# Two load queues, per-bank copies and a moved bias at the start of a squared-ReLU MLP kernel

## The chip, the cores and the metric

One core of one Trainium2 chip runs the whole kernel. The metric is the device time of one execution in microseconds. "Span" is the same execution as the profiler sees it, from the first to the last instruction; it is about 1.8 us shorter than the time. Starts and landings are the trace's; the recorded prediction gives a few of them 0.01 us higher.

## The reference, cut to what matters

```python
# x (1, 2048, 576), w1 (576, 4608), b1 (4608), w2 (4608, 576), b2 (576), all bf16
h = jnp.einsum("bsd,df->bsf", x, w1) + b1
r = jnp.where(h > 0, h, 0)
h = r * r
out = jnp.einsum("bsf,fd->bsd", h, w2) + b2
```

## The kernel before

The kernel works on four blocks of 512 rows. The first product needs x with its 576 columns on the partitions. For the later blocks a transposing DMA brings x in that way. For block 0 there is no time for that, so TensorE itself transposes x. This is the start of the kernel:

```python
WARM = [512] * 6 + [128]                 # matmuls on constants, while the loads run
for i, n in enumerate(WARM):
    keep(nc.tensor.matmul(wps[:, 0:n], lhsT=ones[:, 0:P], rhs=ones[:, 0:n], start=True, stop=True))
# ... (cut)
load_x(nc.sync, 0)                       # x0: 128 rows of x, 144 KB
load_x(nc.scalar, 1)                     # x1
load_w1n(nc.sync, 0)                     # w1k0: 128 rows of w1, the first 512 columns, 128 KB
load_x(nc.scalar, 2)                     # x2
load_w1n(nc.sync, 1)                     # w1k1
load_x(nc.sync, 3)                       # x3
for k in range(2, NK):
    load_w1n(nc.sync, k)                 # w1k2, w1k3
# ... identity; b1 (as 36 rows) and a column of b2 come on GpSimd's own queue; ScalarE's table load (cut)

# order on TensorE in block 0 ("k_outer"):
for j in range(2):                       # x0, x1
    for k in range(NK):
        x_transpose(j, k)
for j in range(2):
    x_transpose(j, NK)
x_copies(0)                              # PSUM -> SBUF, shared by VectorE and ScalarE
part(0, 0)                               # 4 matmuls of 256 columns with w1k0
for k in range(NK + 1):
    x_transpose(2, k)                    # x2
part(0, 1); part(0, 2)                   # w1k1, w1k2
for k in range(NK + 1):
    x_transpose(3, k)                    # x3
x_copies(1)
dup_windows(0)                           # two copies of 64x2048 on VectorE
part(0, 3)                               # w1k3
part(1, 0)
make_b1T()                               # b1 transposed on TensorE
for k in range(1, NK):
    part(1, k)
# ... then 4 matmuls of 64 rows ("pair", tile pn), and the row groups (tile ph), 512 columns each
```

I call the four column slices of w1 w1k0 to w1k3 and the four row tiles of x x0 to x3, as the change does. In the profile the x tiles are `x_sb`, the slices `w1n`, the other pieces of w1 `w_h`, the transposed tiles in PSUM `tb`, the first sums `pn`, and the row groups `ph`.

## Time and profile before

| | before |
|---|---|
| time, median of 3 first runs | 291.02 us (290.59 to 291.36) |
| span of the profiled execution | 289.6 us |
| first transpose / first row-group matmul / last matmul (starts) | 3.77 / 10.29 / 286.66 us |
| clock at full speed from | 6.51 us |

From the page of the kernel before, the header, the busy times and the chain that ended last (its two lines give shares of the span by engine and by source line), then two groups of the start (busy time and mean ns of one, then idle time of the engine before them):

```profile
span 289.6 us, 4693 instructions
PE 285.5 (99%) x2027; PEld 139.9 (48%) x2032; DVE 78.6 (27%) x176; ACT 96.7 (33%) x154; POOL 2.3 (1%) x10
...
PE 98%; DMA 1%; issue 0%; DVE 0%
...
L227 PE MATMUL pn<-xTw,w1n 128*128 128x256 bf16 x32 | 4.6, 295 | 0.0
...
L149 PE MATMUL tb<-ident,x_sb 128*128 128x128 bf16 x20 | 2.4, 288 | 0.2 <-DMA x_sb<-in_x_dram 0.2
```

TensorE is the bound, over the whole span, and the 32 first matmuls (L227) never waited. Busy PE is a weak sign, because matmuls are pipelined and their ends modelled, so I read the starts instead. This is the order in time on PE at the start (start, duration, what, how many; in brackets the idle time before and what ended it):

```profile
3.77 1.25 PE L149 MATMUL tb<-ident,x_sb 128*128 128x128 bf16 x10 [0.17 <-DMA x_sb<-in_x_dram]
4.87 1.01 PE L227 MATMUL pn<-xTw,w1n 128*128 128x256 bf16 x4
5.68 0.74 PE L149 MATMUL tb<-ident,x_sb 128*128 128x128 bf16 x5
6.21 1.19 PE L227 MATMUL pn<-xTw,w1n 128*128 128x256 bf16 x8
7.24 0.44 PE L149 MATMUL tb<-ident,x_sb 128*128 128x128 bf16 x5
7.51 1.04 PE L227 MATMUL pn<-xTw,w1n 128*128 128x256 bf16 x8
8.39 0.22 PE L166 MATMUL b1T_ps<-ident,b_rows 128*128 128x128 bf16 x1
```

After the wait for x0 there is no bracket, so no wait. The single starts behind these lines are 107 ns apart for transposes and 213 ns for 256 columns until 6.51 us, then 56 and 109 ns: the clock doubles. The Trainium skill ("TensorE: Matmul & The Clock Gate", Part 1) says that the clock starts at half speed and is released by a free-running activity window of about 3.4 us. The doubling in this trace agrees.

The loads, from the page (KB each, median us from issue to landing):

```profile
w1n<-in_w_dram SPq DMA_DIRECT2D x4, 128.0 KB, 3.9
x_sb<-in_x_dram ACTq DMA_DIRECT2D x2, 144.0 KB, 2.9
x_sb<-in_x_dram SPq DMA_DIRECT2D x2, 144.0 KB, 3.4
```

The trace's semaphore events give each landing: x1 at 3.52, x0 3.73, x2 4.13, w1k0 4.32, w1k1 5.86, x3 6.07, w1k2 6.47, w1k3 7.05 us.

### The profile page before, as it was taken

To read this page: it belongs to the slowest core of one execution; us is meant where nothing else is said; L and a number is where in the kernel's file an instruction comes from. 1 tells how busy PE (TensorE), PEld (TensorE's weight loads), DVE (VectorE), ACT (ScalarE), POOL (GpSimd) and SP (SyncE) were. 2 spreads that over 40 slices of the span, in tenths; PEclk is the share of its full clock that TensorE was granted. 3 is DMA by queue.
4 is the path that set the end of the run, shared out by engine and by line. 5 is a ranking of instruction groups with operands and counts; after the bars stand their busy time and mean duration, and the time that the engine had idled before them with its cause. 6 is when DMAs were issued, how large, how long until landed. Compare 5 with 4: busy or idle time off the path is not lost.

```text
span 289.6 us, 4693 instructions
## 1 busy us (share of the span) xinstructions
PE 285.5 (99%) x2027; PEld 139.9 (48%) x2032; DVE 78.6 (27%) x176; ACT 96.7 (33%) x154; POOL 2.3 (1%) x10
## 2 busy tenths in 40 slices
PE   8999999999999999999999999999999999999996
PEld 5544444444444555555544444444444455555555
DVE  1644554444500200000015444444440001100001
ACT  2566666666500000000027666666670000000000
POOL 3000000000000000000000000000000000000000
PEclk9999999999999999999999999999999999999999
DMA  7999999400001200000000000000000110000000
GB/s 198 221 245 188 308 389 212 92 0 2 0 14 25 52 16 18 16 16 18 16 16 2 1 2 0 2 0 2 0 2 0 36 38 16 16 16 19 33 16 18
DMA packets 31605, 16.52 MB, mean 57 GB/s; under 512 B 15700, under 2 KB 31584, under 8 KB 31584
## 3 DMA queue, kind: packets, MB, share of 16 engines
q1 hardware_dynamic: 31232, 15.91, 22.3%
q10 hardware_dynamic: 288, 0.30, 0.4%
q8 instruction: 16, 0.26, 0.4%
q14 instruction: 5, 0.04, 0.0%
q0 software_dynamic: 64, 0.01, 0.0%
HBM read 11.36 MB, written 2.36 MB: 47 GB/s over the span
## 4 chain that ended last, share of the span: by engine, by line
PE 98%; DMA 1%; issue 0%; DVE 0%
PE ph L188 42%; PE po L289 38%; PE pt L270 11%; PE pn L209 4%; PE pn L227 1%; DMA x_sb<-in_x_dram 1%; PE tb L149 1%; PE ph L190 1%; PE pn L203 1%; DVE o_sb L291 0%; PE b1T_ps L166 0%; PE pn L205 0%
## 5 line engine op out<-in xcount | busy, mean ns | idle before, releaser
L190 PE MATMUL ph<-xTw,w_h 64*128 64x512 bf16 x576 | 124.6, 376 | 0.0
L188 PE MATMUL ph<-xTw,w_h 64*128 64x512 bf16 x576 | 124.6, 376 | 0.0
L289 PE MATMUL po<-w_sb,hT 128*128 128x448 bf16 (+2 forms) x612 | 109.4, 341 | 0.0
L176 ACT ACTIVATE r<-ph,b1T 128x512 bf16<-128x512 f32 x128 | 81.1, 685 | 41.6 <-PE ph L190 41.6
L188 PEld LDWEIGHTS <-w_h 64*128 64x128 bf16 x576 | 54.1, 94 | 68.3
L289 PEld LDWEIGHTS <-hT 128*128 128x128 bf16 x612 | 58.5, 98 | 51.0
L177 DVE TENSOR_TENSOR hT<-r 128x512 bf16<-128x512 bf16 x144 | 61.2, 426 | 75.9 <-ACT r L176 75.5
L190 PEld LDWEIGHTS <-w_h 64*128 64x128 bf16 x576 | 54.1, 94 | 0.0
L291 DVE TENSOR_TENSOR o_sb<-po,b_bc 128x448 bf16<-128x448 f32 (+2 forms) x17 | 10.2, 597 | 125.8 <-PE po L289 125.8
L270 PE MATMUL pt<-hT,w_sb 128*128 128x512 bf16 x142 | 31.3, 379 | 0.1
L176 ACT ACTIVATE r<-pn,b1T 128x512 bf16<-128x512 f32 x16 | 10.3, 688 | 61.0 <-PE pn L205 59.6
L270 PEld LDWEIGHTS <-w_sb 128*128 128x128 bf16 x144 | 14.1, 98 | 17.0
L273 ACT ACTIVATE oT<-pt,b2T 128x512 bf16<-128x512 f32 x4 | 2.8, 688 | 28.3 <-PE pt L270 28.3
L209 PE MATMUL pn<-xTw,w1n 128*128 128x512 bf16 x45 | 10.4, 379 | 0.4 <-issue 0.3
L209 PEld LDWEIGHTS <-w1n 128*128 128x128 bf16 x48 | 4.5, 98 | 6.0 <-issue 0.8
L227 PE MATMUL pn<-xTw,w1n 128*128 128x256 bf16 x32 | 4.6, 295 | 0.0
L63 PE MATMUL wps<-const-bfloat16-1.0 128*128 128x512 bf16 (+1 forms) x7 | 2.8, 582 | 0.8 <-PEq L344 0.8
L227 PEld LDWEIGHTS <-w1n 128*128 128x128 bf16 x32 | 3.3, 107 | 0.5
L156 DVE COPY xTw<-tb 128x256 bf16<-128x256 bf16 x4 | 1.1, 292 | 6.7 <-PE tb L149 6.7
L119 DVE COPY xTw<-xTw 64x2048 bf16<-64x2048 bf16 x4 | 2.8, 690 | 0.2
L120 DVE COPY xTw<-xTw 64x2048 bf16<-64x2048 bf16 x4 | 2.7, 687 | 0.1
L149 PE MATMUL tb<-ident,x_sb 128*128 128x128 bf16 x20 | 2.4, 288 | 0.2 <-DMA x_sb<-in_x_dram 0.2
(23 smaller groups left out, 15.2 us busy)
## 6 DMA issues: line engine op xcount, KB each, us to landing
w_sb<-in_w_dram SPq DMA_DIRECT2D x4, 1296.0 KB, 12.7
w_h<-in_w_dram SPq DMA_DIRECT2D x14, 288.0 KB, 6.2
out_dram<-o_sb SPq DMA_DIRECT2D x15, 112.0 KB, 1.7
w_h<-in_w_dram SPq DMA_DIRECT2D x4, 144.0 KB, 3.5
w1n<-in_w_dram SPq DMA_DIRECT2D x4, 128.0 KB, 3.9
out_dram<-ot SPq DMA_DIRECT2D x4, 128.0 KB, 2.0
x_sb<-in_x_dram ACTq DMA_DIRECT2D x2, 144.0 KB, 2.9
x_sb<-in_x_dram SPq DMA_DIRECT2D x2, 144.0 KB, 3.4
```

The lines of the kernel that those rows point to most:

```text
L63: keep(nc.tensor.matmul(wps[:, 0:n], lhsT=ones[:, 0:P], rhs=ones[:, 0:n], start=True, stop=True))
L149: keep(nc.tensor.transpose(bank[:, slot, qc], xs[:, j, c0:c0 + P], ident[:]))
L176: keep(nc.scalar.activation(out=r[:], in_=bank[:], func=ACT.Relu, bias=b1T[:, ft:ft + 1], scale=1.0))
L177: keep(nc.vector.tensor_tensor(out=hTs[sb][:, ft, :], in0=r[:], in1=r[:], op=ALU.mult))
L188: keep(nc.tensor.matmul(bx[:], lhsT=w1_h[0:H, LO_C[i], jc], rhs=xT[0:H, LO_W[i], :], start=(i == 0), stop=(i == NC - 1)))
L190: keep(nc.tensor.matmul(by[:], lhsT=w1_h[H:P, UP_C[i], jc], rhs=xT[H:P, UP_W[i], :], start=(i == 0), stop=(i == NC - 1)))
L203: keep(nc.tensor.matmul(banks[2 * i][:], lhsT=w1n8[0:H, i, :], rhs=xT[0:H, SPC, :], start=start, stop=stop, skip_group_check=order == "k_o ...
L209: keep(nc.tensor.matmul(banks[g][:], lhsT=w1n[:, k, g * P:(g + 1) * P], rhs=xT[:, O + k, :], start=start, stop=stop))
L227: keep(nc.tensor.matmul(banks[g][:, hc], lhsT=w1n[:, k, g * P:(g + 1) * P], rhs=xT[:, O + k, hc], start=(h == 0 and k == 0), stop=False, s ...
L270: keep(nc.tensor.matmul(pt[:], lhsT=w2_sb[:, ft, DM:D], rhs=hT[:, ft, :], start=(i == 0), stop=(i == NFT - 1)))
L289: keep(nc.tensor.matmul(po[:, 0:d1 - d0], lhsT=hT[:, ft, jj * P:(jj + 1) * P], rhs=w2_sb[:, ft, d0:d1], start=(i == 0), stop=(i == NFT - 1)))
L291: keep(nc.vector.tensor_tensor(out=o_sb[:, d0:d1], in0=po[:, 0:d1 - d0], in1=b2_bc[:, d0:d1], op=ALU.add))
```

## The change

The intent: let the eight first loads come sooner by issuing them on two queues, with no small transfers among them, and let the copies out of PSUM start as soon as one bank is complete. The core of the diff (renamings, and the plain move of PSUM tiles between pools, are cut):

```diff
-    WARM = [512] * 6 + [128]
+    WARM = [512] * 6 + [256]
...
     load_x(nc.sync, 0)
     load_x(nc.scalar, 1)
-    load_w1n(nc.sync, 0)
-    load_x(nc.scalar, 2)
-    load_w1n(nc.sync, 1)
-    load_x(nc.sync, 3)
-    for k in range(2, NK):
-        load_w1n(nc.sync, k)
+    for k in range(2):
+        load_w1n(nc.sync, k, k + 1)
+        load_x(nc.scalar, 2 + k)
+    load_w1n(nc.sync, 2, 3)
+    load_w1n(nc.scalar, 3, 4)
...
-    nc.gpsimd.dma_start(out=b1_rows[0:NFT, :], in_=b1.rearrange("(ft p) -> ft p", p=P))
-    nc.gpsimd.dma_start(out=b2_col[:], in_=b2[DM:D].rearrange("(d o) -> d o", o=1))
+    keep(nc.scalar.dma_start(out=b1_rows[0:NFT, :], in_=b1.rearrange("(ft p) -> ft p", p=P)))
+    for h in range(2):
+        load_w1n8(nc.sync, h)            # now 64 KB each, whole rows (before: 32 KB in 256-byte pieces)
...
+    def x_transpose(j):                  # tile by tile; two banks per half
+        h, q = divmod(j, 2)
+        hc = slice(h * HS, (h + 1) * HS)
+        for bank, ks in enumerate((T_ORDER[:2], T_ORDER[2:])):
+            for k in ks:
+                # ... transpose into bank
+            for k in ks if q == 1 else ():
+                copy = nc.scalar.copy if h == 1 and k in (2, 3) else nc.vector.tensor_copy
+                keep(copy(...))
...
                 for j in range(2):
-                    for k in range(NK):
-                        x_transpose(j, k)
-                for j in range(2):
-                    x_transpose(j, NK)
-                x_copies(0)
-                part(0, 0)
-                for k in range(NK + 1):
-                    x_transpose(2, k)
-                part(0, 1)
-                part(0, 2)
-                for k in range(NK + 1):
-                    x_transpose(3, k)
-                x_copies(1)
+                    x_transpose(j)
+                for k in range(2):
+                    part(0, k)
+                    x_transpose(2 + k)
                 dup_windows(0)
-                part(0, 3)
+                for k in range(2, NK):
+                    part(0, k)
```

b2's column moves behind the w1 loads on the sync queue, and w2 comes in two loads instead of four.

More of the change, by code (lines that the diff above doesn't have):

```diff
@@ L57 @@
     ps_o = ctx.enter_context(tc.tile_pool(name="ps_o", bufs=4, space=PSUM))
-    wps = ps_o.tile([P, 512], FP32, name="wps", tag="po")
+    wps = ps_h.tile([P, 512], FP32, name="wps", tag="ph")
     ones = nc.const_aps.tensor(1.0, [P, 512], BF16)
-    WARM = [512] * 6 + [128]
+    WARM = [512] * 6 + [256]
     for i, n in enumerate(WARM):
@@ L66 @@
     w1n = wpool.tile([P, NK, GW], BF16, name="w1n")
-    w1n8 = wpool.tile([P, G // 2, P], BF16, name="w1n8")
+    w1n8 = wpool.tile([P, GW], BF16, name="w1n8")
     w1_h = wpool.tile([P, NC, FH], BF16, name="w1_h")
@@ L72, in load_x, with load_w1n @@
         keep(eng.dma_start(out=xs[:, rt, :], in_=x2[rt * P:(rt + 1) * P, :]))
-    def load_w1n(eng, k):
-        keep(eng.dma_start(out=w1n[:, k, :], in_=w1[k * P:(k + 1) * P, 0:GW]))
+    def load_w1n(eng, k0, k1):
+        src = w1[k0 * P:k1 * P, 0:GW].rearrange("(k p) f -> p k f", p=P)
+        keep(eng.dma_start(out=w1n[:, k0:k1, :], in_=src))
     def load_w1n8(eng, h):
-        src = w1[NK * P:D, 0:GW].rearrange("p (i h f) -> p i h f", h=2, f=P)
-        keep(eng.dma_start(out=w1n8[h * H:(h + 1) * H, :, :], in_=src[:, :, h, :]))
+        keep(eng.dma_start(out=w1n8[h * H:(h + 1) * H, :], in_=w1[NK * P:D, 0:GW]))
     def load_w1(eng, h, j0, j1):
@@ L83, in load_w1 @@
                       in_=w1_v[:, :, GW + h * FH + j0 * P:GW + h * FH + j1 * P]))
+    b1_rows = const.tile([P, P], BF16, name="b1_rows")
+    nc.vector.memset(b1_rows[:], 0.0)
     load_x(nc.sync, 0)
     load_x(nc.scalar, 1)
-    load_w1n(nc.sync, 0)
-    load_x(nc.scalar, 2)
-    load_w1n(nc.sync, 1)
-    load_x(nc.sync, 3)
-    for k in range(2, NK):
-        load_w1n(nc.sync, k)
+    for k in range(2):
[3 more added lines that the diff above has]
+    load_w1n(nc.scalar, 3, 4)
     ident = const.tile([P, P], BF16, name="ident")
     make_identity(nc, ident[:])
-    b1_rows = const.tile([P, P], BF16, name="b1_rows")
-    nc.gpsimd.memset(b1_rows[:], 0.0)
-    nc.gpsimd.dma_start(out=b1_rows[0:NFT, :], in_=b1.rearrange("(ft p) -> ft p", p=P))
-    b2_col = const.tile([P, 1], BF16, name="b2_col")
-    nc.gpsimd.dma_start(out=b2_col[:], in_=b2[DM:D].rearrange("(d o) -> d o", o=1))
-    b2T = const.tile([P, 1], FP32, name="b2T")
-    nc.gpsimd.tensor_copy(out=b2T[:], in_=b2_col[:])
     warm = const.tile([P, 1], FP32, name="warm")
     keep(nc.scalar.activation(out=warm[:], in_=nc.const_aps.tensor(0.0, [P, 1], FP32), func=ACT.Relu))
+    keep(nc.scalar.dma_start(out=b1_rows[0:NFT, :], in_=b1.rearrange("(ft p) -> ft p", p=P)))
+    for h in range(2):
+        load_w1n8(nc.sync, h)
     E3, O, SPC, E = 0, 1, 5, 6
@@ L130 @@
     w2_view = w2.rearrange("(ft p) d -> p ft d", p=P)
-    W2CH = 9
+    W2CH = 18
     def load_w2(c):
@@ L140 @@
     HS = SB // 2
-    tb_po = [ps_o.tile([P, 2, HS], BF16, name="tb", tag="po") for _ in range(2)]
-    tb_ph = [ps_h.tile([P, 2, HS], BF16, name="tb", tag="ph") for _ in range(4)]
-    half_banks = [tb_ph, None]
-    def x_transpose(j, k):
+    tb = [[ps_h.tile([P, 4, HS], BF16, name="tb", tag="ph") for _ in range(2)] for _ in range(2)]
+    PLACE = [(0, 0), (0, 1), (1, 0), (1, 1), (1, 2)]
+    T_ORDER = [0, 1, 2, 3, NK]
+    def x_transpose(j):
         h, q = divmod(j, 2)
-        qc = slice(q * P, (q + 1) * P)
-        bank, slot, c0 = (half_banks[h][k], 0, k * P) if k < NK else (half_banks[h][2], 1, D - P)
-        keep(nc.tensor.transpose(bank[:, slot, qc], xs[:, j, c0:c0 + P], ident[:]))
-    def x_copies(h):
         hc = slice(h * HS, (h + 1) * HS)
-        for k in range(NK):
-            src = half_banks[h][k][:, 0, :]
-            if k % 2 == 0:
-                keep(nc.vector.tensor_copy(out=xT0[:, O + k, hc], in_=src))
-            else:
-                keep(nc.scalar.copy(out=xT0[:, O + k, hc], in_=src))
-        keep(nc.vector.tensor_copy(out=xT0[:, E3, hc], in_=half_banks[h][2][:, 1, :]))
+        for bank, ks in enumerate((T_ORDER[:2], T_ORDER[2:])):
+            for k in ks:
+                slot = PLACE[k][1]
+                c0 = k * P if k < NK else D - P
+                keep(nc.tensor.transpose(tb[h][bank][:, slot, q * P:(q + 1) * P], xs[:, j, c0:c0 + P], ident[:]))
+            for k in ks if q == 1 else ():
+                w = O + k if k < NK else E3
+                copy = nc.scalar.copy if h == 1 and k in (2, 3) else nc.vector.tensor_copy
+                keep(copy(out=xT0[:, w, hc], in_=tb[h][bank][:, PLACE[k][1], :]))
     b1T = const.tile([P, NFT], FP32, name="b1T")
     def make_b1T():
-        b1T_ps = ps_o.tile([P, P], BF16, name="b1T_ps", tag="po")
+        b1T_ps = ps_h.tile([P, P], BF16, name="b1T_ps", tag="ph")
         keep(nc.tensor.transpose(b1T_ps[:], b1_rows[:], ident[:]))
@@ L198, in a_full @@
         for g in range(G):
-            pool, tag = (ps_o, "po") if g < 2 else (ps_h, "ph")
+            pool, tag = (ps_o, "po") if g < 2 or order == "k_outer" else (ps_h, "ph")
             banks.append(pool.tile([P, SB], FP32, name="pn", tag=tag))
         def pair(i, start, stop):
-            keep(nc.tensor.matmul(banks[2 * i][:], lhsT=w1n8[0:H, i, :], rhs=xT[0:H, SPC, :],
+            keep(nc.tensor.matmul(banks[2 * i][:], lhsT=w1n8[0:H, 2 * i * P:(2 * i + 1) * P], rhs=xT[0:H, SPC, :],
                              start=start, stop=stop, skip_group_check=order == "k_outer"))
-            keep(nc.tensor.matmul(banks[2 * i + 1][:], lhsT=w1n8[H:P, i, :], rhs=xT[H:P, E3, :],
+            keep(nc.tensor.matmul(banks[2 * i + 1][:], lhsT=w1n8[H:P, (2 * i + 1) * P:(2 * i + 2) * P], rhs=xT[H:P, E3, :],
                              start=start, stop=stop, skip_group_check=order == "k_outer"))
@@ L220, in a_full @@
             if order == "k_outer":
-                tb_new = [ps_h.tile([P, 2, HS], BF16, name="tb", tag="ph") for _ in range(2)]
-                half_banks[1] = tb_new + tb_po
                 def part(h, k):
@@ L231, in a_full @@
                 for j in range(2):
-                    for k in range(NK):
-                        x_transpose(j, k)
-                for j in range(2):
-                    x_transpose(j, NK)
-                x_copies(0)
-                part(0, 0)
-                for k in range(NK + 1):
-                    x_transpose(2, k)
-                part(0, 1)
-                part(0, 2)
-                for k in range(NK + 1):
-                    x_transpose(3, k)
-                x_copies(1)
+                    x_transpose(j)
+                for k in range(2):
+                    part(0, k)
+                    x_transpose(2 + k)
                 dup_windows(0)
-                part(0, 3)
+                for k in range(2, NK):
+                    part(0, k)
                 part(1, 0)
@@ L296 @@
         load_w1(nc.sync, 1, j0, j1)
-        if j0 == 0:
-            load_w1n8(nc.sync, 0)
-            load_w1n8(nc.sync, 1)
     load_xT(1)
@@ L303 @@
         load_w1(nc.sync, 1, j0, j1)
+    b2_col = const.tile([P, 1], BF16, name="b2_col")
+    keep(nc.sync.dma_start(out=b2_col[:], in_=b2[DM:D].rearrange("(d o) -> d o", o=1)))
+    b2T = const.tile([P, 1], FP32, name="b2T")
+    nc.gpsimd.tensor_copy(out=b2T[:], in_=b2_col[:])
     keep(nc.sync.dma_start(out=b2_bc[:], in_=b2.partition_broadcast(P)))
-    for c in (0, 2, 1, 3):
+    for c in range(2):
         load_w2(c)
```

## The prediction

> **What bounds the kernel.** TensorE. The page gives PE busy 285.5 of 289.6 us (99%); the chain of waits is 98% PE; DVE (27%) and ACT (33%) have slack. The matmuls' start times (timeline) show no wait from the first transpose at 3.78 us to the last matmul at 286.7 us, beyond two pauses of 0.1 us where 64-row matmuls take over. The change reorders the first 10 us and some later loads, so it can gain only there.
>
> **The first 10 us before.** x0 is issued at 0.74 and lands at 3.73; transposes start at 3.78. From there PE issues back to back: 20 transposes, 32 matmuls of 256 columns, the bias transpose, the first pair at 9.85. Until 6.52 us matmuls run at half speed (transposes 107 ns apart, 256 columns 213), then at full (56 and 109). The Trainium skill ("TensorE: Matmul & The Clock Gate", Part 1) says a free-running activity window of about 3.4 us releases the clock; the trace agrees in that the rate doubles, 5.7 us after the first warm matmul. The phase should then differ between executions: 1 us more of slow clock costs 0.5, which would explain the 0.8 us spread of the three times.
> Landings against use here: w1k1 5.86 (6.22), x3 6.08 (7.24), w1k2 6.48 (6.80), w1k3 7.05 (7.52). All in time, so earlier loads buy nothing in this execution.
>
> **What the change does.**
> - x3 and w1k3 move to ScalarE's queue (0.44 us per issue): w1k3 is issued near 2.1 instead of 3.13 and should land near 6.0; x3 and w1k1 0.3 to 0.6 earlier. The first four loads are issued as before, so transposes still start at 3.78. Where the clock is released before about 5.4 us, w1k2 and w1k3 would limit the old kernel, and the new one gains up to 0.4.
> - The first bank is complete after the 7th transpose instead of the 5th: the first copy (0.29, DVE) starts 0.2 later, and the first matmul near 5.09 instead of 4.88. At half clock that costs 0.1 to 0.2.
> - All five first-half copies go to DVE (5 x 0.29); only the first is waited for. x3's transposes come a step earlier, so the second half's copies and the two 0.69 us duplications end by 9.8, about when the pair needs them.
> - b1 moves from GpSimd to ScalarE's queue, behind four loads, a 1.28 us table load and a wait for w1k0 (4.33): issue about 4.4, landing 7 to 8 (others issued then took 2.5 to 3.7), needed by PE near 8.5. Thin: PE would stall in order.
> - Last warm matmul 256 columns: ends at 3.5, before x0.
> - w1n8 doubles to 2 x 64 KB; the w1 loads behind it start at nearly the same pace (1 us or more in hand). w2 in two loads: landed by 48, needed at 77.
>
> **Sum.** +0.15 (first copy), -0.2 (average of executions with an early clock), noise: 290.9 us, within 290.3 to 291.5 eight times in ten. Faster by over 2%: 0.01; within 2%: 0.98; slower: 0.01.
>
> **What would show it.** First transpose near 3.78; first 256-column matmul near 5.1; w1k3 landing near 6; b1 landed before its transpose; the pair within 0.3 us of 9.9, allowing for the clock's release; the rest shifted rigidly.
>
> **What would make it wrong.** b1 or the duplications stalling PE (up to 1 us); x0 landing at another time; the extra PE pause moving the clock's release by a whole window (1.7 us); late w1 pieces.

## The result, and the profile after

| | before | after |
|---|---|---|
| time, median of 6 runs | 290.93 us (290.46 to 291.36) | 291.40 us (290.81 to 291.61) |
| ratio | | 1.0014 (95%: 1.0000 to 1.0029): the same |
| span of the profiled execution | 289.6 us | 289.8 us |
| first transpose / first row-group matmul / last matmul (starts) | 3.77 / 10.29 / 286.66 us | 3.50 / 10.60 / 286.97 us |
| clock at full speed from | 6.51 us | 3.56 us |

Ratios are the mean time of one kernel's fast runs over that of the other's of the same rounds, so not quite the ratio of the medians. "The same" means: no difference of 2% or more.

The same parts of the page after:

```profile
span 289.8 us, 4697 instructions
PE 284.9 (98%) x2032; PEld 138.9 (48%) x2032; DVE 78.9 (27%) x179; ACT 95.9 (33%) x152; POOL 0.9 (0%) x7
...
PE 97%; DMA 2%; SPq 0%; DVE 0%; issue 0%
...
L217 PE MATMUL pn<-xTw,w1n 128*128 128x256 bf16 x32 | 4.1, 273 | 1.5 <-DMA w1n<-in_w_dram 1.4
```

The group of the first matmuls now has 1.5 us of idle time before it, nearly all of it for a load of w1. The order in time on PE shows where:

```profile
3.50 0.76 PE L149 MATMUL tb<-ident,x_sb 128*128 128x128 bf16 x10
5.68 0.61 PE L217 MATMUL pn<-xTw,w1n 128*128 128x256 bf16 x4 [1.42 <-DMA w1n<-in_w_dram]
6.13 0.44 PE L149 MATMUL tb<-ident,x_sb 128*128 128x128 bf16 x5
6.66 0.61 PE L217 MATMUL pn<-xTw,w1n 128*128 128x256 bf16 x4
7.11 0.44 PE L149 MATMUL tb<-ident,x_sb 128*128 128x128 bf16 x5
7.39 1.47 PE L217 MATMUL pn<-xTw,w1n 128*128 128x256 bf16 x12
8.70 0.22 PE L159 MATMUL b1T_ps<-ident,b_rows 128*128 128x128 bf16 x1
```

Ten transposes took 0.76 us instead of 1.25, because the clock was already at full speed. Then PE stood still until w1k0 came. From the start of x2's last transpose at 6.35 to 6.66 is 0.31 us where 0.06 is the plain distance: a second, smaller wait, for w1k1. The chain of waits leads through w1k1, which was issued at 1.68 (start, duration, what):

```profile
1.68 4.93 DMA w1n<-in_w_dram
6.61 0.05 issue
6.66 0.61 PE pn L217 x4
```

The loads:

```profile
x_sb<-in_x_dram ACTq DMA_DIRECT2D x3, 144.0 KB, 4.2
w1n<-in_w_dram SPq DMA_DIRECT2D x3, 128.0 KB, 5.0
x_sb<-in_x_dram SPq DMA_DIRECT2D x1, 144.0 KB, 2.7
```

Each load took longer from issue to landing, except x0 and x1. (The medians 4.2 and 5.0 stand where 2.9 and 3.9 stood, but x3 and w1k3 have changed queues, so they are not of the same loads; x2 alone took 4.25 us instead of 2.97.) Landings: x1 3.23, x0 3.41, x2 5.41, w1k0 5.63, x3 6.40, w1k1 6.61, w1k3 6.97, w1k2 7.17 us. So the last landing of the eight was at 7.17 instead of 7.05, though the last issue was at 2.16 instead of 3.12.

The difference of the two executions can be balanced, as an estimate. A transpose that starts 0.27 sooner gains 0.27. The clock before ran at half speed for 6.51 - 3.77 = 2.74 us of work, after for 0.06; half of the difference, 1.34 us, is gained. Take both from 10.29 and the first row group would start at 8.68; it started at 10.60, so 1.92 us were lost again. Some 1.5 us of this are waits for loads: the first copy was over at 4.42 us but w1k0 landed at 5.63, and w1k1 cost another 0.25. The other 0.4 us I have not broken down. Net +0.31, and the last matmul is 0.31 later. The two executions differ by luck (the clock) and by loads, and one pair can't say how much of the second is luck too. That is what the experiments are for.

### The profile page after: what moved, and what is told of

Read it like the earlier page. It is cut to its first block, busy times and chain, and to the rows that moved or that the text cites. A ratio compares the mean times of both kernels' runs of the same rounds, so it can differ in the third digit from the quotient of the medians.

```text
span 289.8 us, 4697 instructions
## 1 busy us (share of the span) xinstructions
PE 284.9 (98%) x2032; PEld 138.9 (48%) x2032; DVE 78.9 (27%) x179; ACT 95.9 (33%) x152; POOL 0.9 (0%) x7
## 4 chain that ended last, share of the span: by engine, by line
PE 97%; DMA 2%; SPq 0%; DVE 0%; issue 0%
PE ph L181 42%; PE po L271 38%; PE pt L252 11%; PE pn L202 4%; DMA w1n<-in_w_dram 2%; PE pn L217 1%; PE ph L183 1%; PE pn L196 1%; SPq L76 0%; SPq L72 0%; DVE o_sb L273 0%; PE tb L149 0%; PE b1T_ps L159 0%; PE pn L198 0%
## 5 line engine op out<-in xcount | busy, mean ns | idle before, releaser
L153 DVE COPY xTw<-tb 128x256 bf16<-128x256 bf16 x8 | 1.9, 284 | 5.8 <-PE tb L149 5.4
L198 PE MATMUL pn<-xTw,w1n 64*128 64x512 bf16 x8 | 2.4, 379 | 0.0
```

## The experiments

Three theories. **Queue theory**: loads on two queues at once get in each other's way, so those needed first land later. **Chance theory** (also called stall theory): landings scatter in any kernel, and so does the clock. **Copy theory**: the later first copy costs the time. A fourth, the **table theory** (ScalarE's table load holds up the loads), came up on the way. The runs e1 to e4 used one chip, d1 to d4 a second and h1 to h4 a third; each ratio compares executions of one chip.

In all tables, "T" is the start of the first transpose, "ph" that of the first row-group matmul, in us from the span's start.

### e1: the kernel before once more

No edit.

> The kernel before, unchanged, as a second look at its first 10 us. Queue theory (the new kernel is late because x3 and w1k3, issued early on a second queue, share the DMA engines with x2 and w1k0): here w1k0 again lands near 4.3 us and x2 near 4.1, no wait of PE for w1k0. Stall theory (one DMA engine stalls for about 1 us at a random moment in any kernel): in this second trace w1k0 or x2 may land 1 us or more later or earlier than the 4.33 and 4.13 of the first. Clock theory (the release of the clock falls at a free phase between about 3.3 and 6.7 us): the release is not again at 6.5. Time ratio 1.000, 95% within 0.0015.

Measured: ratio 1.0005 (0.9993 to 1.0017) for identical code, which is the size of what can be told by time alone. The clock was released at 4.86 us, not 6.51. T 3.45, ph 9.44, w1k0 at 4.35, x2 4.53, last of the eight loads at 6.19 (7.05 in the first look). PE waited for no load of w1. So the clock theory holds in this second look. x2 and w1k0 landed as the queue theory expects, within 0.4 us of the first look and not 1 us off as the stall theory allowed; but landings of the later loads scatter by nearly 1 us in one and the same kernel.

### e2: the new kernel with the loads put back

```diff
-    for k in range(2):
-        load_w1n(nc.sync, k, k + 1)
-        load_x(nc.scalar, 2 + k)
-    load_w1n(nc.sync, 2, 3)
-    load_w1n(nc.scalar, 3, 4)
+    load_w1n(nc.sync, 0, 1)
+    load_x(nc.scalar, 2)
+    load_w1n(nc.sync, 1, 2)
+    load_x(nc.sync, 3)
+    for k in range(2, NK):
+        load_w1n(nc.sync, k, k + 1)
```

> The new kernel with only the queues and the order of the eight x and w1 loads put back (x3 and w1k3 on the sync queue again). Queue theory: w1k0 lands near 4.3 again, the first 256-column matmul starts at 4.4 to 5.1 instead of 5.68, and the time falls to that of the kernel before or a little above (ratio 0.999 to 1.001). Stall theory: w1k0 lands anywhere from 4.3 to 5.7, ratio as of the full change, 1.0014. Copy theory (the later first copy costs the time): first matmul 0.2 us or more after w1k0 has landed, ratio 1.0005 to 1.001.

Measured: median 290.86 us, ratio 1.0006 (0.9993 to 1.0019). Clock from 5.31 us; w1k0 at 4.39, last of the eight at 6.16 (w1k3 was issued only at 3.44, because its completion semaphore was still in use by x1, which landed at 3.42). The start in time, of this kernel:

```profile
3.64 1.25 PE L150 MATMUL tb<-ident,x_sb 128*128 128x128 bf16 x10
3.81 1.21 SPq L79 DMA_DIRECT2D w1n<-in_w_dram  x2
4.58 0.15 PEld L218 LDWEIGHTS <-w1n 128*128 128x128 bf16 x1
4.61 1.08 DVE L154 COPY xTw<-tb 128x256 bf16<-128x256 bf16 x5 [3.68 <-PE tb L150]
4.95 0.75 PE L218 MATMUL pn<-xTw,w1n 128*128 128x256 bf16 x4
```

and the same piece of the unchanged kernel in e1:

```profile
3.45 1.25 PE L149 MATMUL tb<-ident,x_sb 128*128 128x128 bf16 x10
3.60 1.40 SPq L82 DMA_DIRECT2D w_h<-in_w_dram  x2
4.20 0.29 DVE L156 COPY xTw<-tb 128x256 bf16<-128x256 bf16 x1 [4.20 <-PE tb L149]
```

The first copy starts 4.61 - 3.64 = 0.97 us after the first transpose, against 4.20 - 3.45 = 0.75; the first matmul follows at 1.31 us instead of 1.10. So the per-bank copy delays the first matmul by 0.2 us where w1k0 is there in time. By the first row group this delay can no longer be told (the column "rest" of the table below: 5.28 us here, 5.29 in e1, 5.15 in the first look). The queue theory's numbers came (w1k0 at 4.39), and the copy theory's sign too, but the time is not told from that of the unchanged kernel.

### e3: the kernel before with only the new queues

```diff
-    load_w1n(nc.sync, 0)
-    load_x(nc.scalar, 2)
-    load_w1n(nc.sync, 1)
-    load_x(nc.sync, 3)
-    for k in range(2, NK):
-        load_w1n(nc.sync, k)
+    for k in range(2):
+        load_w1n(nc.sync, k)
+        load_x(nc.scalar, 2 + k)
+    load_w1n(nc.sync, 2)
+    load_w1n(nc.scalar, 3)
```

> The kernel before with only the new queues and order of the eight loads. Queue theory: w1k0 lands at 5 us or later, PE waits 0.5 to 1.5 us for it after the transposes, w1k3 lands no earlier than 6.5, ratio 1.001 to 1.002. Stall theory: landings scatter as in the kernel before, ratio 1.000. My prediction's view (w1k3 near 6.0, first four loads unchanged): ratio 0.999.

Measured: median 291.31 us, ratio 1.0014 (1.0000 to 1.0027). w1k0 landed at 4.20, so the queue theory in the form that I had written (w1k0 itself late) fell. What was late were w1k2 (7.17, issued at 2.14) and w1k3 (7.35, issued at 2.16). The clock was released only at 6.78, and yet PE had to wait: the chain of waits of this kernel leads through one load from 2.14 to 7.17 us (start, duration, what):

```profile
2.14 5.03 DMA w1n<-in_w_dram
7.17 0.05 issue
7.22 0.61 PE pn L226 x4
```

### e4: the kernel before with only the bias loads moved

```diff
-    nc.gpsimd.memset(b1_rows[:], 0.0)
-    nc.gpsimd.dma_start(out=b1_rows[0:NFT, :], ...)
-    nc.gpsimd.dma_start(out=b2_col[:], ...)
+    nc.vector.memset(b1_rows[:], 0.0)                        # ahead of the loads
+    keep(nc.scalar.dma_start(out=b1_rows[0:NFT, :], ...))    # after ScalarE's table load
+    keep(nc.sync.dma_start(out=b2_col[:], ...))              # behind the w1 loads
```

> The kernel before with only the bias loads moved: b1 on ScalarE's queue, b2's column later on the sync queue, nothing on GpSimd's software queue. If the small pieces slow the loads beside them (w1k1 landed 1.5 us after w1k0 in the kernel before): w1k1 lands near 5.0 instead of 5.86 and the ratio is 0.999 or a little less. If they don't: w1k1 again at 5.5 to 6.0, ratio 1.000 within 0.0007. b1 lands before its transpose at 8 us or later, no wait for it.

Measured: median 291.10 us, ratio 1.0012 (1.0000 to 1.0024). w1k1 landed at 4.70 and not at 5.86, as the small-piece idea expects, but in e1, with the small pieces in place, it landed at 5.06, and the time did not fall. So taking the small pieces out shows no gain. This kernel had the earliest start of the row groups (ph 9.38, clock from 4.33), and lost 0.29 us of it again by the last matmul: 276.66 us after ph, where most kernels have 276.37. The trace shows why: at 13.55 us a weight load waited for one of the later pieces of w1, which landed at 13.51 where it had landed at 12.86 in e1.

```profile
PEld L186 <- DMA w_h<-in_w_dram: 0.4, 1, 0.4
```

So an earlier start of the row groups can run into the next loads, and part of what it gained is lost there.

### The six starts, side by side

As an estimate, half the time between T and the clock's release is what half speed costs; the rest of the way from T to ph is PE's own work at full clock plus waits.

| trace | loads | clock from | T | ph | half speed costs | rest | last of eight loads |
|---|---|---|---|---|---|---|---|
| before | old | 6.51 | 3.77 | 10.29 | 1.37 | 5.15 | 7.05 |
| e1 | old | 4.86 | 3.45 | 9.44 | 0.70 | 5.29 | 6.19 |
| e2 | old | 5.31 | 3.64 | 9.75 | 0.83 | 5.28 | 6.16 |
| e4 | old | 4.33 | 3.55 | 9.38 | 0.39 | 5.45 | 6.28 |
| after | new | 3.56 | 3.50 | 10.60 | 0.03 | 7.07 | 7.17 |
| e3 | new | 6.78 | 3.76 | 10.72 | 1.51 | 5.46 | 7.35 |

Two things stand out. The release came anywhere from 3.56 to 6.78 us, worth up to 1.5 us of time; this alone hides a difference of 0.4. And the two traces with the new queues have the latest last loads. (The clock records, which 12 of the 14 traces have, bear out the free-running window: they hold full speed for 283.31, 286.72 or 290.13 us, lengths that lie 3.41 us apart and are 83, 84 and 85 times 3.41.)

### d1 to d4: the clock taken out of the comparison

To remove the clock's chance, I held the whole start back by about 4 us in four kernels, with warm matmuls running meanwhile, so that the clock is at full speed before the first transpose. The edit, the same for the four (for the two kernels that come from the new one, a gate tile stands for b1_rows):

```diff
-    WARM = [512] * 6 + ...
+    WARM = [512] * 17 + ...
+    for _ in range(3):
+        keep(nc.vector.memset(xs[:], 0.0))                                  # the x loads must wait for this
+    keep(nc.gpsimd.tensor_copy(out=b1_rows[:], in_=xs[:, 0, 0:P]))          # GpSimd and its b1 load too
     load_x(nc.sync, 0)
```

In the kernels that come from the one before, b2's small piece is not held back (in d1 it is issued at 1.3 us), so it is out of the way here.

d1 is the held-back kernel before:

> The kernel before with its whole start held back about 4 us: 17 warm matmuls, and the x loads wait for three fills of their tile, so that the clock is at full speed before the first transpose in every execution. This takes the clock's free phase out of the comparison. Time about 3 us over the kernel before (ratio near 1.010); spread of the executions below the 0.8 us of the undelayed kernel if the clock made that spread (clock theory), as wide if DMA landings made it. All loads land as long after x0's issue as before: w1k3 5.4 to 6.3 us after it, first row-group matmul 8.3 to 9.1 us after it, bound by w1k2 and w1k3.

d2 is the held-back new kernel:

> The new kernel held back in the same way. Queue theory (loads on two queues land later as a group): last of the eight loads 6.3 to 6.6 us after x0's issue, first row-group matmul 0.3 to 1.0 us later than in the held-back kernel before, and the time with it. Chance theory (the difference of the two kernels came from the clock's phase in the executions that were timed): same within 0.2 us. My prediction's view: 0.3 us faster, since w1k3 lands 1 us sooner.

d3 is the new kernel with the old loads (as e2), held back:

> The held-back new kernel with the eight loads in the old queues and order. Queue theory: time as the held-back kernel before, within 0.2 us, or a little less since nothing is on the software queue. Copy theory: 0.2 us or more above the held-back kernel before, with the first matmul waiting for the first copy and not for w1k0.

d4 is the kernel before with the new loads (as e3), held back:

> The held-back kernel before with only the new queues and order of the eight loads. Queue theory: 0.3 to 1.0 us above the held-back kernel before, w1k2 or w1k3 landing 6.3 us or more after x0's issue with PE waiting for it. Chance theory: within 0.2 us of it.

Measured, all executions in us (+ marks those with a mean granted clock of 0.994 instead of 0.999 or 1.000; 0.6% of 293 us is 1.8 us, an estimate, so their lateness is in part or wholly the clock's):

| | loads | executions | ratio to the kernel before |
|---|---|---|---|
| d1 | old | 294.97, 295.05, 295.09, 295.95 | 1.0148 (1.0135 to 1.0161) |
| d3 | old | 294.90, 295.04, 295.08, 295.33, 296.87+ | 1.0159 (1.0139 to 1.0179) |
| d2 | new | 294.91, 294.98, 296.05, 296.08 | 1.0156 (1.0141 to 1.0172) |
| d4 | new | 295.12, 295.22, 296.40, 296.58, 297.12+, 297.91+ | 1.0187 (1.0162 to 1.0212) |

The executions fall into an early group near 295.0 us, the same for all four kernels, and late ones about 1 us or more above it. The clock theory's expectation that the spread would shrink with the clock out fell (d1: 0.98 us); what is left is, as far as the traces tell, the scatter of the landings. The copy theory fell too: d3 has the new copies, yet its median is that of d1 (295.08 and 295.07 us) where 0.2 us more was expected. Two more misses: the delay cost 4.3 us and not 3 (ratio 1.0148, not 1.010), and d1's wait is for w1k0, not for w1k2 or w1k3. d2's trace came as the queue theory expected (last landing 6.59 us after x0's issue, first row group 0.99 us later than in d1 counted from there), but it is of one of the two late executions; d4's did not (last landing 5.40 us after x0's issue, not 6.3), but it is of an early one (295.12). At full clock PE now waits for loads of w1 or x in every one of these traces. The waits of PE (total, times, longest), for the held-back kernel before and then for the held-back new kernel, whose traced execution was a late one:

```profile
PE pn L229 <- DMA w1n<-in_w_dram: 1.0, 1, 1.0
PE wps L63 <- PEq L346: 0.8, 1, 0.8
PE tb L151 <- DMA x_sb<-in_x_dram: 0.4, 1, 0.4
```

```profile
PE pn L221 <- DMA w1n<-in_w_dram: 1.6, 2, 1.4
PE wps L63 <- PEq L331: 0.8, 1, 0.8
PE tb L153 <- DMA x_sb<-in_x_dram: 0.3, 1, 0.3
```

The traces' packet records show what a late landing is. A load goes out in 128 packets of 1 KB or so, spread over the 16 DMA engines; a packet usually takes 51 ns (1152 bytes) or 46 ns (1024). Some 2 to 4 us after x0's issue a few packets take far longer: in d2 up to 1147 ns, in the first trace of the new kernel up to 1004 ns. The pieces of a load then land far apart (w1k0 in that trace: first piece 3.74, last 5.63 us; before: 3.93 and 4.32). In that trace 12 of w1k0's 16 pieces had landed by 4.12; and of each of the four loads behind it 12 or 13 pieces landed within 1 us and the last three or four trailed, 0.2 to 0.5 us apart. That looks as if engines that were late stayed late, but the packet records don't name the engine, so it is not shown.

### h1 to h4: more executions, and two more rivals

h1 repeats d1, and h2 repeats d2, for the counts. h3 tests a rival that the traces suggested: in the new kernel ScalarE's table load comes after four issues, at 1.9 to 3.2 us after the first issue, just where packets stalled. Its edit, in the held-back new kernel:

```diff
+    keep(nc.scalar.activation(out=warm[:], ..., func=ACT.Relu))   # table load at 0.73 us
     for _ in range(3):
...
-    keep(nc.scalar.activation(out=warm[:], ..., func=ACT.Relu))   # behind the loads
```

(the activation stands right ahead of the loads in the program, and waits for nothing). h4 puts all eight loads of the held-back new kernel on the sync queue, in the same order:

```diff
-    load_x(nc.scalar, 1)
+    load_x(nc.sync, 1)
     for k in range(2):
         load_w1n(nc.sync, k, k + 1)
-        load_x(nc.scalar, 2 + k)
+        load_x(nc.sync, 2 + k)
     load_w1n(nc.sync, 2, 3)
-    load_w1n(nc.scalar, 3, 4)
+    load_w1n(nc.sync, 3, 4)
```

> The held-back kernel before once more, for the count of late executions. So far its executions fell into an early group near 295.0 us and a late one near 296 (1 of 4 late). Queue theory (two queues at once make single DMA packets stall for about 1 us or more, and every load is spread over all engines, so all later loads wait): at most 2 of 5 above 295.5, longest packet between 2 and 5 us after x0's issue below 0.9 us. Chance theory: as many late ones as in the held-back new kernel.

> The held-back new kernel once more (2 of 4 late so far). Queue theory and table theory alike: half or more of the executions above 295.5 us, and in a late one a packet of 0.9 us or longer within 2 to 4 us of x0's issue. Chance theory: 1 in 4 or 5.

> The held-back new kernel with ScalarE's table load moved to the very start, 4 us before the loads. In the new kernel the table load lies at 1.9 to 3.2 us after x0's issue, where the packets stalled; in the kernel before it was over by 2.2. Table theory (the table load holds up packets): no packet of 0.9 us, executions all near 295.0 us. Queue theory: still half or more above 295.5.

> The held-back new kernel with all eight loads on the sync queue in the same order (x1 is then issued 0.45 us later, w1k3 some 3.3 us after x0; the table load too is over early, since ScalarE issues none of them). Queue theory: no packet of 0.9 us, at most 1 execution in 5 more than 0.5 us above the lowest; the level itself 0.2 to 0.6 us above 295.0, because the issues follow each other on one sequencer. If packets stall as long with one queue, the queue theory falls.

Measured:

| | loads | executions | above 295.5 us | longest packet of the eight loads, 2 to 5 us after the first issue |
|---|---|---|---|---|
| h1 | old | 294.98, 295.09, 295.41, 295.87, 296.14 | 2 of 5 | 753 ns |
| h2 | new | 294.88, 295.33, 295.41, 295.77, 296.28, 297.88+ | 3 of 6 | 968 ns |
| h3 | new, early table | 294.71, 294.79, 294.85, 295.55, 295.80, 295.96 | 3 of 6 | 704 ns |
| h4 | one queue | 295.79, 296.49, 296.75, 297.01, 297.02 | 5 of 5 | 664 ns |

- The table theory fell: with the table load long over (2.0 us, loads from 4.8), 3 of 6 executions were late as before. That its trace has no packet of 0.9 us (704 ns) was what the table theory expected, but it is one trace, of an early execution. Its early level is perhaps 0.1 us lower (three executions at 294.71 to 294.85); I do not build on that.
- h1 and h2 gave what the queue theory expected, but just so. All held-back executions together: old loads 4 late of 14 (d1, d3, h1), new loads 12 late of 22 (d2, d4, h2, h3). The means are 295.41 and 295.80 us. The excess points to the new queues, yet if both had the same odds, a split at least this uneven would come up about 1 time in 8 (counting the ways to place 16 late ones among 36). Four of the late ones are the + executions; without them it is 3 of 13 and 9 of 19, means of 295.30 and 295.51 us, and about 1 time in 6. On the h chip alone it is 2 of 5 and 6 of 12, and the times there no longer fall into two groups. So it is suggested and not shown.
- The longest packets divide more clearly, though the line at 900 ns was drawn after the e and d traces, and of the h traces h2 fits it and h3 doesn't. With the new loads 4 of 6 traces have one above 900 ns (after 1004, e3 1069, d2 1147, h2 968; d4 271 and h3 704 do not), with the old loads none of 7 (before 654, e1 553, e2 548, e4 369, d1 751, d3 680, h1 753), and with one queue not either (664). A long packet does not by itself make an execution late: h2's 968 ns are from one of 295.33 us.
- h4 was a poor test of the times. No long packet came, as the queue theory expects, but its level was 1.7 us up where I had expected 0.2 to 0.6, and 4 of 5 executions lay more than 0.5 us above the lowest where at most 1 was expected, because the queue was now so late that the other pieces of w1 behind it arrived late as well. Its waits of PE show them as w_h; from the first row group to the last matmul it took 278.02 us instead of 276.37:

```profile
PE ph L187 <- DMA w_h<-in_w_dram: 0.8, 1, 0.8
...
PE pn L221 <- DMA w1n<-in_w_dram: 0.6, 2, 0.3
PE tb L153 <- DMA x_sb<-in_x_dram: 0.5, 2, 0.3
```

One result does not depend on counting late executions. It is when the last of the eight loads landed, counted from the first issue (x0 on the sync queue, or x1 on ScalarE's, which comes 0.35 us sooner in the held-back traces):

| | traces | last landing, us after the first issue | mean |
|---|---|---|---|
| old loads | before, e1, e2, e4, d1, h1, d3 | 6.31, 5.45, 5.43, 5.55, 5.94, 6.75, 6.04 | 5.93 |
| new loads | after, e3, d2, h2, d4, h3 | 6.43, 6.62, 6.95, 5.99, 5.75, 5.68 | 6.24 |

The last issue came about 1.1 us sooner with the new queues (1.64 us after the first, mean, against 2.70), the last landing no sooner. In the 3 us from 2 to 5 us after the first issue the eight loads moved 282 GB/s with the old queues and 298 with the new (means of the same traces). So the last landing did not follow the issuing here. In these 3 us the packets took 0.88 to 1.02 of the 16 DMA engines' time (13 traces), so the engines had little room; but why they moved no more is open, for with packets of the same size (1152 bytes) they moved 389 GB/s from 36.2 to 43.4 us of the kernel before. The Trainium skill ("DMA: Bandwidth & Descriptors", "Issuing engines are not separate DMA queues") says that DMAs of different issuing engines share the same 16 DMA engines, and that issuing from several saves only the sequencer's time. These landings agree.

No experiment pointed to a version that beats both kernels, so none was run. All of the start is worth little: from e4, the earliest start seen, to e3, the latest, the first row group moves by 1.34 us, 0.5% of the time, and most of that (1.12 us by the table) is the clock.

## Why the prediction was right or wrong, point by point

- **The time, and "within 2%": right.** 290.9 with 290.3 to 291.5 was predicted, 291.40 measured. The main step held: TensorE bounds the span, and once the first row group starts the rest shifts rigidly (276.37 us to the last matmul in 11 of 14 traces, before and after the change). That the range was hit does not vouch for the small terms: of the two in the sum, one failed and the other can't be told at the first row group. With terms of 0.2 us and a range of 1.2, the hit is owed to the rigid rest of the kernel, and in part to luck.
- **The clock's free phase as the cause of the spread: right for the undelayed kernels** in that releases came at 3.56, 4.33, 4.86, 5.31, 6.51 and 6.78 us. It is not the only cause: with the clock at full speed before the first transpose (d and h runs) the times still spread by 1 us and more.
- **"w1k3 is issued near 2.1 instead of 3.13 and should land near 6.0; x3 and w1k1 0.3 to 0.6 earlier": this step failed.** The issue was right (2.12 in the trace), the landing was 6.97; x3 landed at 6.40 instead of 6.07 and w1k1 at 6.61 instead of 5.86. I had taken an earlier issue for an earlier landing. The eight loads moved about as much per us from either set of queues (282 and 298 GB/s), and single late packets came on top.
- **"The first four loads are issued as before, so transposes still start at 3.78": half right.** They were issued as before, but x0 landed at 3.41, and x2 and w1k0 1.3 us later than in the first look. x0's landing scatters in the unchanged kernel too (3.73, 3.40).
- **"Where the clock is released before about 5.4 us, w1k2 and w1k3 would limit the old kernel, and the new one gains up to 0.4": this step failed.** In e1 and e4, with releases at 4.86 and 4.33 us, PE waited for neither of them, because they landed sooner too (6.19 us or before in e1, 6.28 in e4). The new kernel's profiled execution had the earliest clock of the six undelayed traces, and it lost 1.92 us by the estimate above, some 1.5 of it to loads: with an early clock PE is sooner done with what it has, and the loads become the bound. This was the -0.2 of the sum.
- **The first copy +0.2 us: right for the first matmul**, 0.21 us later in e2 against e1; at the first row group it can't be told. In the profiled execution after the change it is hidden behind the wait for w1k0.
- **b1 and the duplications: right**, with no stall. b1's transpose started 109 ns after the matmul before it, the plain distance. Of the risks that I named, two came: "x0 landing at another time" (3.41) and "late w1 pieces" (w1k0 and w1k1 above). Of the signs that I named, the first transpose (3.50, not 3.78), the first 256-column matmul (5.68, not 5.1) and w1k3 (6.97, not 6) missed.
- **The sum's sign was wrong by a little.** -0.05 was the net of the sum, 1.0014 of 291 is +0.4, with an interval from 0 to 0.8. The experiments do not settle how much of this is the queues: e3 gave 1.0014, e2 without them 1.0006, but e4 1.0012 and the identical kernel 1.0005.

What stays open: why single packets take 1 us, and whether two queues make them longer or I have seen too few traces.

## What to carry to other kernels

Issuing loads sooner on a second queue bought nothing here, since issuing did not limit them: compare bytes moved per us and the landing of the last load, not the issue times. A load counts only when its last piece has landed, and in these traces one load's pieces came up to 2.1 us apart, so judge a reordering by many executions. And before comparing two starts of a few us, read off where the clock was released in each: that alone can be worth more than the change.

## What the Trainium skill lacked or had wrong

- "TensorE: Matmul & The Clock Gate", Part 1, puts the transition around 4 us into sustained activity, give or take 500 ns. Here it came 2.8 to 6.0 us after the first warm matmul at 0.78 us (releases at 3.56 to 6.78 us, in six traces of nearly the same start). A spread of 3.2 us fits a free-running window of about 3.4 us, as the page describes it; its 500 ns do not. Nor was a whole window of matmuls needed: the earliest release came 2.79 us after the first one.
- "DMA: Bandwidth & Descriptors" has no number for how long single packets take when they take far longer than the rest. Here packets of 1 KB that usually took 46 to 51 ns took up to 1147 ns in the first 5 us of loading, and one 128 KB load had its first piece landed at 3.74 and its last at 5.63 us.
